# Dealing the bias generator's relu planes anew between two engines, and loading and casting the second unit's q, k and v later

## The chip, the cores and the metric

The kernel runs on one core of a Trainium2 chip. The metric is the device time of one execution in microseconds, given as the median of three runs. Five engines work side by side, each through its own instructions in order: PE (matrix multiply and transpose), DVE (vector), ACT (activation functions and copies), POOL (general) and SP (which here issues every DMA). Two engines meet only at semaphores: an instruction that waits holds up all that stands behind it on its engine.

## What is computed

For 4 batches and 8 heads, with 576 positions and 64 features a head, the reference computes attention with a learned relative bias, and then a two-layer network on the result:

```python
scores = scale * np.matmul(q, k.transpose(0, 1, 3, 2))
x = (np.log1p(np.abs(rel)) / psi_i)[..., None]
h = np.maximum(x @ w1 + b1, 0.0)
bias = h @ w2
scores = scores + bias.transpose(2, 0, 1)[None, :, :, :]
attn = softmax(scores)
y = attn @ v
g = leaky_relu(y @ w_in)
out = g @ w_out
```

The bias depends on positions and heads alone: it is made once, at the start, and serves all four batches.

## The kernel before

The work has three stages. The **generator** makes the bias rows in 36 tiles of 16 rows of positions (the list `GEN` is their order). A tile needs four *relu planes* of 304 to 576 columns. `gen_r` makes each plane on ACT or on DVE (L113, L115), as the string `plan[g]` says; `plan` is worked out ahead by a loop that gives each plane to the engine with the smaller running load (L93 to L103). The planes live in a ring of nine buffers (tag `r`), so a plane can be begun only once the plane nine places before it has gone through PE. `gen_mm` multiplies the four planes with the second layer's weights on PE (L126), `gen_ev` scales the product into an SBUF row tile with two ACT instructions (L133, L134) and has SP write it to one of five DRAM tensors (L145). `gen_tick` runs the three in a staggered way. After certain tiles it calls `load_bias`, which reads a finished group of rows back as the bias of 128 query positions (L164 to L170); the last group, "3", is read when all rows are written.

The **attention** stage goes over 16 units (a pair of heads and a batch), with nine tiles each, in the order `KINDS` = A0 B0 A1 B1 M A2 B2 A3 B3. `step(n)` issues tile n: the scores on PE (`qk_mm`), the sum with the bias and the row's extreme on DVE (L265, `softmax_a`), exp on ACT (L273), and, three tiles later, transposes of the probabilities (L307), copies of them (L323, L316) and the product with v (L342, `pv`). After tiles M and B3 `recip` takes the reciprocal of the sums on DVE (L279, L280) and spreads it on POOL (L283 to L286). Unit 0 multiplies q and k as they are loaded (L236). Every later unit multiplies split values (L242): `split_hi` casts q and k on DVE (L195, L200), `split_lo` takes the rest on POOL (L207, L210), q in two halves and k in two halves; the first two matmuls of a tile use q and the cast k, the last two the rest of k. The table `SPL` says behind which tile of unit u the pieces for unit u + 1 are issued. `load_unit(u)` has SP load q and k (two halves each, L180), `load_v(u)` v (L186, L188); units 0 and 1 are loaded at the start of the program (L501 to L503), unit u + 2 from within unit u.

The third stage is the network (L461 to L497). No scheduler moves anything: each engine gets its instructions in the order in which the program issues them. SP's are in one queue, with the waits on semaphores in place.

Of the kernel before, what the change touches and what calls it, by code (L numbers as in the profile page):

```python
# [25 lines left out]
KINDS = ["A0", "B0", "A1", "B1", "M", "A2", "B2", "A3", "B3"]  # L26
GEN = [16, 17] + list(range(16)) + [34, 35] + list(range(18, 26)) + list(range(33, 25, -1))
SPL = {1: [(0, "q")], 2: [(1, "q", 0)], 3: [(1, "q", 1)], 4: [(0, "k")], 5: [(1, "k", 0)], 7: [(1, "k", 1)]}
GEN_AT = [39] * 9
LAG = 3  # L30
BLK = 512
# [5 lines left out]
def attention_ffn(ctx: ExitStack, tc: tile.TileContext, qt, kt, vm, vt, wi, wo, cst, out):  # L37
# [39 lines left out]
    def gen_setup():  # L77
        cut = 214 + S - 16 * GEN[0]
        for c in (slice(0, cut), slice(cut, 214 + S)):
            nc.sync.dma_start(out=cs[:, c], in_=cst[:, c])  # L80
        nc.vector.memset(warm[:], 0.0)
        nc.scalar.activation(out=warm[:], in_=warm[:], func=AF.Exp)
        nc.vector.tensor_scalar(out=bps[:], in0=psib, scalar1=b1c, scalar2=None, op0=ALU.mult)
        for c in (slice(0, cut - 214), slice(cut - 214, S)):
            nc.vector.tensor_scalar(out=ltw[:, c], in0=ltw[:, c], scalar1=w1c, scalar2=None, op0=ALU.mult)
        nc.gpsimd.tensor_scalar(out=w2d, in0=w2d, scalar1=8.0, scalar2=None, op0=ALU.mult)
# [3 lines left out]
    def gen_w(T):  # L90
        return max(S - 16 * T, 16 * T + 16)

    plan, load = [], {"a": 0.0, "v": 5.0}  # L93
    for T in GEN:
        w = gen_w(T)
        load["a"] += 0.84
        cost = {"a": 0.24 + 0.00072 * w, "v": 0.11 + 0.00056 * w}
        eng = ""
        for _ in range(4):
            e = min(cost, key=lambda c: load[c] + cost[c])  # L100
            load[e] += cost[e]
            eng += e
        plan.append("".join(sorted(eng)))  # L103

    def gen_r(g):
        T = GEN[g]
        w = gen_w(T)
        r = gr[T] = [None] * 4
        for q, c in enumerate(plan[g]):
            k = 4 * T + q  # L110
            t = gp.tile([128, S], F32, tag="r", name="r", bufs=9)
            if c == "a":
                nc.scalar.activation(out=t[:, :w], in_=ltw[:, :w], func=AF.Relu, bias=bps[:, k:k + 1])  # L113
            else:
                nc.vector.tensor_scalar(out=t[:, :w], in0=ltw[:, :w], scalar1=bps[:, k:k + 1], scalar2=0.0, op0=ALU.add, op1=ALU.max)  # L115
            r[q] = t

    def gen_mm(T):
        r = gr.pop(T)
        w = gen_w(T)  # L120
        pt = pstile("s" if w > 512 else "to"[T % 2])
        cuts = [(0, w)] if w <= 512 else [(0, w // 2), (w // 2, w)]
        o0 = 512 - w // 2 if w > 512 else 0
        for a, b in cuts:
            for q in range(4):
                nc.tensor.matmul(pt[32 * q:32 * q + 32, o0 + a:o0 + b], w2d, r[q][:, a:b], start=True, stop=True)  # L126
        gps[T] = pt, o0

    def gen_ev(T):
        pt, o0 = gps.pop(T)  # L130
        R, F = 16 * T + 15, S - 16 * T
        e = e_b[GEN.index(T) % len(e_b)]
        nc.scalar.activation(out=e[:, R:W], in_=pt[:, o0:o0 + F], func=AF.Copy, scale=ips[:, T:T + 1])  # L133
        nc.scalar.activation(out=e[:, 0:R], in_=pt[:, o0 + R:o0:-1], func=AF.Copy, scale=ips[:, T:T + 1])  # L134
        if T < 16:
            c, r0 = str(T // 8), 16 * (T % 8)
        elif T < 18:
            c, r0 = "M", 16 * (T - 16)
        elif T < 34:
            c, r0 = str(2 + (T - 18) // 8), 16 * ((T - 18) % 8)  # L140
        else:
            c, r0 = "M", 32 + 16 * (T - 34)
        a = r0 * H * PIT + 1
        dst = scr[c][a:a + 16 * (H * PIT + 1)].rearrange("(i x) -> i x", i=16)[:, 0:H * PIT].rearrange("i (h p) -> i h p", h=H)[:, :, 0:W]
        nc.sync.dma_start(out=dst, in_=e)  # L145

    def gen_tick(g):
        if g + 1 < 36:
            gen_r(g + 1)
        if 0 <= g < 36:  # L150
            gen_mm(GEN[g])
        if 0 <= g - 1 < 36:
            gen_ev(GEN[g - 1])
        for c in {16: "0", 24: "1", 27: "M", 34: "2", 37: "3"}.get(g, ()):
            load_bias(0, c)

    bias = {}

    def load_bias(hp, c):
        n = 64 if c == "M" else 128  # L160
        rows = scr[c][0:n * H * PIT].rearrange("(i h p) -> i h p", h=H, p=PIT)[:, :, 16:16 + S]
        if c == "M":
            t = ap.tile([128, S], F32, tag="biasM", name="biasM", bufs=2)
            nc.sync.dma_start(out=t[0:64, :], in_=rows[:, 2 * hp, :])  # L164
            nc.sync.dma_start(out=t[64:128, :], in_=rows[:, 2 * hp + 1, :])
        else:
            t = ap.tile([128, 2, S], F32, tag="bias", name="bias", bufs=5)
            nc.sync.dma_start(out=t[:, 0, :], in_=rows[:, 2 * hp, :])
            nc.sync.dma_start(out=t[:, 1, 64:S], in_=rows[:, 2 * hp + 1, 0:512])
            nc.sync.dma_start(out=t[:, 1, 0:64], in_=rows[:, 2 * hp + 1, 512:S])  # L170
        bias[hp, c] = t
# [3 lines left out]
    def load_unit(u):  # L175
        hp, b = divmod(u, B)
        q_, k_ = raw_b[u % 2] if u else raw_0
        for t, src in ((q_, qt), (k_, kt)):
            for p in (0, 64):
                nc.sync.dma_start(out=t[p:p + 64], in_=src[hp, b])  # L180
        raw[u] = (q_, k_)

    def load_v(u):
        hp, b = divmod(u, B)
        v_ = ap.tile([128, 4, 128], F32, tag="v", name="v", bufs=3)
        nc.sync.dma_start(out=v_[:], in_=vm[hp, b])  # L186
        for h in range(2):
            nc.sync.dma_start(out=vt_b[u % 3][64 * h:64 * h + 64, h, :], in_=vt[hp, b, h])  # L188
        vv[u] = v_
# [200 lines left out]
    def w_alloc(pool, m):  # L390
        wt[m] = [pool.tile([128, DM], F32R, name=f"w{c}{m}") for c in ("ih", "il", "oh", "ol")]

    def x_alloc(pool, i):
        for k in range(KC):
            xs[i, k] = [pool.tile([128, BLK], F32R, name=f"x{c}{i}{k}") for c in "hl"]
# [102 lines left out]

    with tc.manual_schedule():
        gen_setup()  # L500
        for u in range(2):  # L501
            load_unit(u)
            load_v(u)  # L503
        done = -1
        early_ops = []
        for n in range(NTILE + LAG + 6):
            u, i = divmod(n, 9)
            if u == 0:
                while done < GEN_AT[i]:
                    gen_tick(done)  # L510
                    done += 1
            if n == 9:
                gen.close()
                early = ctx.enter_context(tc.tile_pool(name="early", bufs=1, side="right"))
                x_alloc(early, 0)
                w_alloc(early, 0)
                early.tile([128, 24], F32, name="gap")
                stage, stage_y = ExitStack(), ExitStack()
                pools["s"] = stage.enter_context(tc.tile_pool(name="stage", bufs=1, side="right"))
                pools["y"] = stage_y.enter_context(tc.tile_pool(name="stage_y", bufs=1, side="right"))  # L520
            step(n)
            if n == 13:
                w_fill()
                for m in range(EARLY):
                    early_ops += [(w_abs, m, h) for h in range(2)]
                    early_ops += [(w_bits, m, h, k) for k in range(4) for h in range(2)]
                    if m == 0:
                        early_ops += [(w_hi, 0, h) for h in range(2)] + [(w_lo, 0, h, nc.vector) for h in range(2)]
            for _ in range({0: 3, 4: 3}.get(i, 0) if n >= 18 else 0):
                if early_ops:  # L530
                    f, *args = early_ops.pop(0)
                    f(*args)
            if n == NTILE + 2:
                ffn1(0, 0)
            if u < HP * B:
                if u % B == B - 1 and u // B + 1 < HP:
                    c = {1: "0", 2: "1", 3: "M", 4: "2", 6: "3"}.get(i)
                    if c:
                        load_bias(u // B + 1, c)
                if u + 1 < HP * B:  # L540
                    for f, *args in SPL.get(i, ()):
                        (split_hi, split_lo)[f](u + 1, *args)
                if i == 8 and u + 2 < HP * B:
                    load_v(u + 2)
# [97 lines left out]
```

## Time and profile before

| | |
|---|---|
| median of 3 runs | 703.01 us (702.84 to 703.58) |
| the profiled execution | 702.97 us |
| its span, first to last instruction | 701.2 us |
| PE busy, share of the span | 691.4 us, 99% |
| weight loads of PE busy | 542.1 us, 77% |
| DVE busy | 368.2 us, 53% |
| ACT busy | 362.9 us, 52% |
| POOL busy | 109.9 us, 16% |

Between the span and the time lie 1.8 us that belong to no instruction. The shares are means over three stages with different limits, so each stage has to be read by itself: the generator fills about the first 50 us, the attention ends near 305 us, and the rest is the network. A busy PE is one whose matmuls overlap in the records, not one that runs at its peak. What counts for an engine in order is what its waiting instruction waits for, and what stands behind it.

### The profile page before, as it was taken

To read this page: it belongs to the slowest core of one execution; us is meant where nothing else is said; L and a number is where in the kernel's file an instruction comes from. 1 tells how busy PE (TensorE), PEld (TensorE's weight loads), DVE (VectorE), ACT (ScalarE), POOL (GpSimd) and SP (SyncE) were. 2 spreads that over 40 slices of the span, in tenths; PEclk is the share of its full clock that TensorE was granted. 3 is DMA by queue.
4 is the path that set the end of the run, shared out by engine and by line. 5 is a ranking of instruction groups with operands and counts; after the bars stand their busy time and mean duration, and the time that the engine had idled before them with its cause. 6 is when DMAs were issued, how large, how long until landed. Compare 5 with 4: busy or idle time off the path is not lost.

```text
span 701.2 us, 11179 instructions
## 1 busy us (share of the span) xinstructions
PE 691.4 (99%) x4192; PEld 542.1 (77%) x4192; DVE 368.2 (53%) x872; ACT 362.9 (52%) x792; POOL 109.9 (16%) x139
## 2 busy tenths in 40 slices
PE   7999999999999999999999999999999999999997
PEld 3446788777877778768888888888888888888896
DVE  6997788988898898569993111121111211111211
ACT  8998878787788777765653212222122222222221
POOL 0005434543454345100000000000000000000000
PEclk9999999999999999999999999999999999999999
DMA  9996779548738752005540100001000010000100
GB/s 230 338 303 191 206 185 241 141 109 231 205 98 246 217 145 73 1 1 156 175 121 1 60 1 0 1 1 60 1 0 1 1 60 1 0 1 1 60 1 31
DMA packets 30262, 68.26 MB, mean 97 GB/s; under 512 B 8192, under 2 KB 8320, under 8 KB 30208
## 3 DMA queue, kind: packets, MB, share of 16 engines
q1 hardware_dynamic: 30208, 67.54, 33.5%
q8 instruction: 33, 0.54, 0.3%
q14 instruction: 21, 0.17, 0.1%
HBM read 51.92 MB, written 15.61 MB: 96 GB/s over the span
## 4 chain that ended last, share of the span: by engine, by line
PE 95%; DMA 1%; ACT 1%; DVE 1%; issue 0%; SPq 0%; DVEq 0%
PE ps_o L461 14%; PE ps_t L461 13%; PE ps_o L342 12%; PE ps_s L242 10%; PE ps_s L489 9%; PE ps_s L488 9%; PE ps_s L487 9%; PE ps_t L307 9%; PE ps_o L126 2%; PE ps_t L126 2%; PE ps_s L227 1%; PE ps_s L126 1%; PE ps_o L296 1%; PE ps_o L325 1%; ACT r L113 1%; DMA scr<-x 1%
## 5 line engine op out<-in xcount | busy, mean ns | idle before, releaser
L476 DVE TENSOR_TENSOR gl<-g,gh 128x512 fp32r<-128x512 f32 (+1 forms) x80 | 51.0, 638 | 266.2 <-ACT g L470 266.2
L489 PE MATMUL ps_s<-woh,gl 128*128 128x512 f32 x288 | 112.2, 389 | 0.3 <-DVE gl L476 0.3
L487 PE MATMUL ps_s<-woh,gh 128*128 128x512 f32 x288 | 112.3, 390 | 0.0
L488 PE MATMUL ps_s<-wol,gh 128*128 128x512 f32 x288 | 112.2, 390 | 0.0
L265 DVE CUSTOM_DVE_ANT_0 p<-ps_s,bias 128x576 f32<-128x576 f32 x128 | 94.4, 753 | 30.4 <-PE ps_s L242 26.7
L273 ACT ACTIVATE p<-p,mx 128x576 f32<-128x576 f32 x128 | 99.8, 779 | 5.5 <-DVE mx L265 4.8
L323 ACT COPY PT<-ps_t 128x512 f32<-128x512 f32 x128 | 73.8, 577 | 47.5 <-PE ps_t L307 47.5
L242 PE MATMUL ps_s<-ks,qs 128*128 128x288 f32 x480 | 93.7, 317 | 0.2 <-DVE mx L265 0.2
L469 ACT ACTIVATE gh<-ps_o 128x512 fp32r<-128x512 f32 (+1 forms) x39 | 21.5, 552 | 126.5 <-PE ps_o L461 126.5
L469 ACT ACTIVATE gh<-ps_t 128x512 fp32r<-128x512 f32 (+1 forms) x39 | 21.5, 551 | 112.0 <-PE ps_t L461 111.9
L242 PEld LDWEIGHTS ps_s<-ks,qs 128*128 128x128 f32 x480 | 67.6, 189 | 13.6 <-issue 6.1
L307 PE MATMUL ps_t<-ident,p 128*128 128x128 f32 x512 | 77.5, 274 | 0.0
L342 PE MATMUL ps_o<-PT,v 128*64 128x288 f32 x512 | 69.2, 412 | 0.0
L307 PEld LDWEIGHTS ps_t<-ident,p 128*128 128x128 f32 x512 | 61.0, 140 | 9.1 <-issue 8.2
L489 PEld LDWEIGHTS ps_s<-woh,gl 128*128 128x128 f32 x288 | 54.1, 188 | 11.9 <-DVE gl L476 0.7
L488 PEld LDWEIGHTS ps_s<-wol,gh 128*128 128x128 f32 x288 | 54.1, 188 | 10.8
L487 PEld LDWEIGHTS ps_s<-woh,gh 128*128 128x128 f32 x288 | 54.1, 188 | 10.7
L461 PE MATMUL ps_t<-xh,wil 128*128 128x512 f32 (+1 forms) x156 | 57.3, 367 | 0.0
L461 PE MATMUL ps_o<-xh,wil 128*128 128x512 f32 (+1 forms) x156 | 57.3, 367 | 0.0
L461 PE MATMUL ps_o<-xl,wih 128*128 128x512 f32 (+1 forms) x156 | 57.3, 367 | 0.0
L461 PE MATMUL ps_t<-xl,wih 128*128 128x512 f32 (+1 forms) x156 | 57.3, 367 | 0.0
L461 PE MATMUL ps_o<-xh,wih 128*128 128x512 f32 (+1 forms) x156 | 57.3, 367 | 0.0
(111 smaller groups left out, 1081.4 us busy)
## 6 DMA issues: line engine op xcount, KB each, us to landing
raw<-kt SPq DMA_DIRECT2D x32, 304.0 KB, 5.9
raw<-qt SPq DMA_DIRECT2D x32, 288.0 KB, 4.4
raw<-wi SPq DMA_DIRECT2D x16, 512.0 KB, 4.9
raw<-wo SPq DMA_DIRECT2D x16, 512.0 KB, 3.6
scr<-x SPq DMA_DIRECT2D x21, 295.5 KB, 4.6
bias<-scr SPq DMA_DIRECT2D x16, 288.0 KB, 4.6
out<-x SPq DMA_DIRECT2D x18, 256.0 KB, 2.1
v<-vm SPq DMA_DIRECT2D x16, 256.0 KB, 5.7
```

The lines of the kernel that those rows point to most:

```text
L242: nc.tensor.matmul(s_[:, S0 + HS * hh:S0 + HS * hh + HS], qs[:, c0:c0 + 128], ks[:, k0 + HS * hh:k0 + HS * hh + HS], start=(j == 0), stop= ...
L265: nc.vector.tensor_tensor_reduce(out=p, in0=s_[:, S0:S0 + S], in1=bt, scale=-0.125, scalar=3.4e38, op0=ALU.add, op1=ALU.min, accum_out=i)
L273: nc.scalar.activation(out=p, in_=p, func=AF.Exp, bias=i, scale=-1.0, accum_out=sm)
L307: nc.tensor.transpose(t0[:, 128 * jb:128 * jb + 128], p[:, p0 + 128 * jb:p0 + 128 * jb + 128], ident[:])
L323: nc.scalar.copy(out=PT[:, g, 0:8, c].rearrange("p (j h) c -> p j h c", h=2)[:, :, h, :], in_=t0[:].rearrange("p (j c) -> p j c", j=4))
L342: nc.tensor.matmul(o[64 * h:64 * h + 64, 0:HS], l, r, start=(jb == 0), stop=(jb == 4))
L461: nc.tensor.matmul(h_[:, :N], w, x[:, :N], start=(j == 0), stop=(j == len(mms) - 1))
L469: nc.scalar.activation(out=gh[:, :N], in_=h_[:, :N], func=AF.Prelu, alpha=0.01)
L476: nc.vector.tensor_sub(gl[:, :N], g[:, :N], gh[:, :N].bitcast(F32))
L487: nc.tensor.matmul(o, gh[:, c], wt[m][2][:], start=(m == 0), stop=False)
L488: nc.tensor.matmul(o, gh[:, c], wt[m][3][:], start=False, stop=False)
L489: nc.tensor.matmul(o, gl[:, c], wt[m][2][:], start=False, stop=(m == MF - 1))
```

## The change

It makes three edits. The planner's start loads and costs are given other numbers, and so other planes go to ACT and to DVE. Unit 1 is no longer loaded at the start: its `load_unit` and `load_v` are called in the generator's tick 37, behind the reading of bias group "3". And while unit 0 runs, a table `SPL1` takes the place of `SPL`: q's cast is issued behind tile M (index 4), the first half of q's rest and k's cast behind A2 (5), the second half of q's rest behind B2 (6), both halves of k's rest behind A3 (7).

```diff
 SPL = {1: [(0, "q")], 2: [(1, "q", 0)], 3: [(1, "q", 1)], 4: [(0, "k")], 5: [(1, "k", 0)], 7: [(1, "k", 1)]}
+SPL1 = {4: [(0, "q")], 5: [(1, "q", 0), (0, "k")], 6: [(1, "q", 1)], 7: [(1, "k", 0), (1, "k", 1)]}
...
-    plan, load = [], {"a": 0.0, "v": 5.0}
+    plan, load = [], {"a": -1.6, "v": 0.0}
     for T in GEN:
         w = gen_w(T)
-        load["a"] += 0.84
-        cost = {"a": 0.24 + 0.00072 * w, "v": 0.11 + 0.00056 * w}
+        load["a"] += 0.80
+        cost = {"a": 0.187 + 0.00083 * w, "v": 0.11 + 0.00057 * w}
...
         for c in {16: "0", 24: "1", 27: "M", 34: "2", 37: "3"}.get(g, ()):
             load_bias(0, c)
+        if g == 37:
+            load_unit(1)
+            load_v(1)
...
-        for u in range(2):
-            load_unit(u)
-            load_v(u)
+        load_unit(0)
+        load_v(0)
...
-                    for f, *args in SPL.get(i, ()):
+                    for f, *args in (SPL if u else SPL1).get(i, ()):
                         (split_hi, split_lo)[f](u + 1, *args)
```

The diff shows the numbers of the planner and not the deal that comes of them. DVE now makes 117 of the 144 planes (115 before), ACT 27 (29 before). The first planes on DVE, at the start of the program, where `r` is a plane and the last number its columns. Before:

```order
L85 TENSOR_SCALAR cs<-cs 128x256
L115 TENSOR_SCALAR r<-cs,bps 128x304
L115 TENSOR_SCALAR r<-cs,bps 128x576 x3
L115 TENSOR_SCALAR r<-cs,bps 128x560 x3
L115 TENSOR_SCALAR r<-cs,bps 128x544 x3
```

Now:

```order
L86 TENSOR_SCALAR cs<-cs 128x256
L116 TENSOR_SCALAR r<-cs,bps 128x320
L116 TENSOR_SCALAR r<-cs,bps 128x304 x4
L116 TENSOR_SCALAR r<-cs,bps 128x576 x3
L116 TENSOR_SCALAR r<-cs,bps 128x560 x3
L116 TENSOR_SCALAR r<-cs,bps 128x544 x4
```

Four of the small planes of the first two tiles, and one of 544 columns, have gone from ACT to DVE; later tiles give planes back.

SP's queue around the end of the generator. `scr_76` holds the rows of group "3", `raw_84` and `raw_85` are the buffers of unit 1's q and k, `raw_82` and `raw_83` those of unit 2. Before:

```order
L145 DMA scr_76<-x_2_71 16x8x591 [waits DMAHW5_49,Activation_49]
L145 DMA scr_76<-x_3_72 16x8x591 [waits DMAHW6_49,Activation_49]
L168 DMA bias<-scr_76 128x576 [waits DMAHW6_49,DMAHW5_49,DMAHW7_49,DMAHW1_49,DMAHW0_49]
L169 DMA bias<-scr_76 128x512
L170 DMA bias<-scr_76 128x64
L180 DMA raw_82<-qt 64x1152 [waits DMAHW2_49]
L180 DMA raw_82<-qt 64x1152 [waits DMAHW3_49]
L180 DMA raw_83<-kt 64x1216 [waits DMAHW4_49]
```

Now:

```order
L146 DMA scr_76<-x_2_71 16x8x591 [waits DMAHW6_49,Activation_49]
L146 DMA scr_76<-x_3_72 16x8x591 [waits DMAHW7_49,Activation_49]
L172 DMA bias<-scr_76 128x576 [waits DMAHW6_49,DMAHW2_49,DMAHW7_49,DMAHW1_49,DMAHW0_49]
L173 DMA bias<-scr_76 128x512
L174 DMA bias<-scr_76 128x64
L184 DMA raw_84<-qt 64x1152 [waits DMAHW3_49]
L184 DMA raw_84<-qt 64x1152 [waits DMAHW4_49]
L184 DMA raw_85<-kt 64x1216 [waits DMAHW5_49]
L184 DMA raw_85<-kt 64x1216
L190 DMA v<-vm 128x512
```

Unit 1's loads stand directly behind the reading of group "3", whose first instruction waits for the landing of the group's writes; that is the place that unit 2's loads had. Unit 2's follow behind unit 1's.

DVE from tile M of unit 0 on. The ISA rows are the sum with the bias and its extreme, `qs` and `ks` the cast q and k. Before:

```order
L265 ISA pM,mx<-ps_s,biasM 128x576 [waits DMAHW2_49,DMAHW1_49,PE_49]
L265 ISA mx 128x1
L200 CAST ks_782<-raw_85 128x1216
L265 ISA p,mx<-ps_s,bias 128x576 [waits DMAHW2_49,PE_49]
L265 ISA mx 128x1
L279 TENSOR_SCALAR sm<-sm 128x5 [waits Activation_49]
L280 RECIPROCAL sm<-sm 128x5 [waits DVE_49]
```

Now:

```order
L269 ISA pM,mx<-ps_s,biasM 128x576 [waits DMAHW3_49,DMAHW2_49,PE_49]
L269 ISA mx 128x1
L199 CAST qs_101<-raw_84 128x1024 [waits DMAHW4_49,DMAHW3_49]
L269 ISA p,mx<-ps_s,bias 128x576 [waits PE_49]
L269 ISA mx 128x1
L283 TENSOR_SCALAR sm<-sm 128x5 [waits Activation_49]
L284 RECIPROCAL sm<-sm 128x5 [waits DVE_49]
L204 CAST ks_821<-raw_85 128x1216 [waits DMAHW6_49,DMAHW5_49]
```

q's cast stood between tiles B0 and A1 and now stands between M and A2. It has got a wait for the landing of two DMAs, which are q's two halves. k's cast has got such a wait too. On POOL the spreading of M's reciprocal now comes ahead of q's rest, where it came behind it.

## Rows read from the trace of the kernel before

**Rows 1.** Busy time by stretch: us, then PE, PEld, DVE, ACT, POOL, clock, DMA share, GB/s.

```profile
61.00:76.60 15.60, 15.60 (x128) 12.21 (x128) 12.36 (x33) 12.04 (x30) 6.48 (x10) 1.00 0.77 182
76.60:92.20 15.60, 15.60 (x129) 12.20 (x128) 12.22 (x35) 12.90 (x30) 7.25 (x10) 1.00 0.67 194
```

**Rows 2.** The chain of waits behind the generator: start, length, what.

```profile
52.76 4.00 DMA scr<-x
...
56.91 2.86 DMA bias<-scr
...
59.91 0.76 DVE p L265
...
60.73 0.79 PE ps_s L242 x4
```

**Rows 3.** DVE's relu planes as one group: busy, mean ns, idle time before them.

```profile
L115 DVE TENSOR_SCALAR r<-cs,bps 128x560 f32<-128x560 f32 (+17 forms) x115 | 42.0, 450 | 2.9 <-PE ps_t L126 1.4 <-PE ps_s L126 1.1 <-PE ps_o L126 0.3
```

**Rows 4.** DVE's timeline in the generator: start, length, idle time before in brackets.

```profile
5.97 1.41 DVE L115 TENSOR_SCALAR r<-cs,bps 128x576 f32<-128x576 f32 x3 [1.43 <-PE ps_t L126]
...
10.22 38.79 DVE L115 TENSOR_SCALAR r<-cs,bps 128x544 f32<-128x544 f32 x108 [1.13 <-PE ps_s L126]
```

**Rows 5.** ACT's timeline: the generator's last eviction.

```profile
50.31 0.61 ACT L134 ACTIVATE x<-ps_t,cs 128x431 f32<-128x431 f32 x1
```

**Rows 6.** SP's timeline of issues, from the last two writes on.

```profile
52.13 1.17 SPq L145 DMA_DIRECT2D scr<-x  x2
...
58.24 1.15 SPq L180 DMA_DIRECT2D raw<-qt  x2
59.43 1.24 SPq L180 DMA_DIRECT2D raw<-kt  x2
```

**Rows 7.** DMA issues, each second half: KB, us from the issue's start to landing.

```profile
raw<-qt SPq DMA_DIRECT2D x1, 288.0 KB, 5.1
...
raw<-kt SPq DMA_DIRECT2D x1, 304.0 KB, 6.5
```

**Rows 8.** DVE's timeline in unit 0.

```profile
52.10 0.69 DVE L195 CAST qs<-raw 128x1024 fp32r<-128x1024 f32 x1
52.70 0.75 DVE L265 CUSTOM_DVE_ANT_0 p<-ps_s,bias 128x576 f32<-128x576 f32 x1
...
54.30 0.76 DVE L265 CUSTOM_DVE_ANT_0 pM<-ps_s,biasM 128x576 f32<-128x576 f32 x1 [0.16 <-PE ps_s L227]
...
56.88 0.17 DVE L279 TENSOR_SCALAR sm<-sm 128x5 f32<-128x5 f32 x1
```

**Rows 9.** POOL's timeline: the rest of q, the spreading, the rest of k.

```profile
52.93 2.51 POOL L207 TENSOR_TENSOR qs<-raw,qs 64x512 fp32r<-64x512 f32 x2 [48.88 <-DVE qs L195]
57.41 0.40 POOL L283 COPY rb<-sm 128x256 f32<-128x256 f32 x1 [1.98 <-DVE sm L280]
...
58.18 2.92 POOL L210 TENSOR_TENSOR ks<-raw,ks 128x576 fp32r<-128x576 f32 x2
...
74.74 1.43 POOL L210 TENSOR_TENSOR ks<-raw,ks 128x576 fp32r<-128x576 f32 x1
```

**Rows 10.** PE's timeline: first matmuls; scores of A3 of unit 0, of B0 of unit 1.

```profile
4.68 2.13 PE L126 MATMUL ps_t<-r,cs 128*32 128x320 f32 x7 [4.68 <-ACT r L113]
...
57.51 0.76 PE L236 MATMUL ps_s<-raw,raw 64*128 64x288 f32 x4
...
64.58 0.79 PE L242 MATMUL ps_s<-ks,qs 128*128 128x288 f32 x4
```

**Rows 11.** One matmul form from 7.9 to 9.9 us and from 28.5 to 30 us.

```profile
L126 PE MATMUL ps_s<-r,cs 128*32 128x288 f32 x16 | 2.5, 687 | 0.0
...
L126 PE MATMUL ps_s<-r,cs 128*32 128x288 f32 x5 | 1.2, 416 | 0.0
```

**Rows 12.** Busy time by stretch behind the last matmul; the clock follows POOL.

```profile
697.60:699.00 1.40, 0.00 (x0) 0.00 (x0) 0.03 (x1) 0.59 (x1) 0.00 (x0) 1.00 0.36 133
699.00:701.00 2.00, 0.00 (x0) 0.00 (x0) 0.00 (x0) 0.00 (x0) 0.00 (x0) 0.75 0.45 169
```

## The prediction

> **What bounds the kernel now.** I read the busy times by stretch first, to find where PE sets the pace, then the chain of waits for what holds it up before that, and then the timeline of each engine on that chain.
>
> From 61 us on PE leaves no gap: two units in a row take 15.6 us each and PE is busy for all of both, while DVE and ACT have some 3 us of slack in each [rows 1]. What PE has to do from there to the end is the same in both kernels, so the end moves by as much as PE's place at the start of unit 1 moves, unless a new wait appears later. That place is the scores of unit 1's first tile, at 60.73 [rows 2]. Ahead of it the chain runs through the generator's last write (52.76, 4.00 long), the reading of bias group "3" behind its landing (56.91), and tile A3 on DVE at 59.91 [rows 2]. So what matters is what the change does to two things: the generator's end, and everything that DVE, POOL and PE need before unit 1.
>
> **The generator (the new deal).** DVE makes 115 planes in 42.0 us and is idle for 2.9 us between them [rows 3], all of it before 10.22; from there 108 planes follow each other without a gap for 38.79 us, 0.36 us a plane [rows 4]. ACT's last eviction ends at 50.92 [rows 5], behind DVE's last plane at 49.0. With the new deal DVE has four planes more at once and works where it stood idle. Of the 2.9 us I leave some 0.8: the ring of nine still holds its first 576-column plane until the first plane has gone through PE, at 5.97 [rows 4], and four small planes more bring DVE only to about 5.6; and about 0.4 us more where PE, slow at that time (below), is late again. The two planes that DVE makes more in all cost 0.7 us. The gain is 2.9 - 0.8 - 0.7 = 1.4 us at DVE's end, and I carry it to ACT's last eviction, the last write and the reading of group "3". Bounds: 0.5 us, if PE and ACT hold the ring up more often, and 2.2 us, if no idle time is left.
>
> Taking unit 1's seven transfers out of SP's queue at the start saves nothing that I can see: there are 19 row tiles, so no eviction waits for a write before the 20th. Were a late write what holds that one up, the transfers' 1.5 MB would be worth some tenths.
>
> **The loads.** This is the costly edit. SP issues in order, and group "3" waits for the landing of the last write: the last two writes are issued at 52.13, the next issue is at 56.91 [rows 2, 6]. Whatever stands behind it cannot leave earlier. In the kernel before that place belongs to unit 2's q and k, so their rows tell when unit 1's will land. q's second half is issued at 58.24 + 1.15 / 2 = 58.8 and lands 5.1 us later, at 63.9; k's second half is issued at 60.05 and lands 6.5 us later, at 66.55 [rows 6, 7]. With the gain of 1.4 us that is 62.5 and 65.15. Before, the same data had been there since the start and its cast ran at 52.10 without a wait [rows 8].
>
> **The casts.** DVE now meets q's cast directly behind tile M. M is done at 55.0 [rows 8]; without q's cast ahead of it (0.6 us) and with the gain it is done near 53.0. There DVE stands for 62.5 - 53.0 = 9.5 us, and behind it tiles A2, B2, A3 and B3, on which ACT and PE wait. PE has the scores of two tiles ahead, no more, since it has two score buffers.
>
> From q's landing on, in the times of the kernel before (the gain comes off at the end):
>
> - q lands at 63.9; cast 0.6 (52.10 to 52.70, rows 8): 64.5.
> - A2's sum and extreme, 0.7 (a reduction is 0.75 with some overlap, rows 8): 65.2.
> - M's reciprocal, from 56.88 on DVE to 57.41 on POOL, 0.5 [rows 8, 9]: 65.7.
> - The spreading on POOL, 57.41 to 58.18, 0.8 [rows 9]: 66.5. It now stands ahead of q's rest in POOL's queue.
> - q's rest, both halves, 2.5 [rows 9]: 69.0.
> - The first half of k's rest, 1.4 [rows 9]: 70.4. k's cast fits beside: k lands at 66.55 and a cast of some 1.1 us ends before 69.0.
>
> Then PE can begin the second pair of matmuls of unit 1's first tile. Before, it did so in the middle of the 0.79 us that begin at 60.73, at 61.1. So PE's place moves by 70.4 - 61.1 = 9.3 us, less 1.4: **7.9 us later**. PE's other work up to there, tiles A3 and B3 and their transposes, fits into the time in which POOL works, if the clock is full. The products with v and the next tiles then run at the old pace; unit 2's loads, now behind unit 1's, land some 6 us later than before and are needed 8 us later, so they bring no second stall.
>
> **PE's clock.** PE will do nothing for about 9 us. That is far longer than anything inside the old kernel. The old trace shows both ends of the matter: the same 288-column matmul takes 687 ns at 8 us, 3 us behind the first matmul at 4.68, and 416 ns at 29 us [rows 10, 11], and behind the last matmul (ended 697.6) the granted clock is still 1.00 until 699 and 0.75 on average over the next two microseconds, that is 1.2 GHz for half of them [rows 12]. So I take it that PE comes back at 1.2 GHz when A2 frees its buffer, near 63.8, and is at 2.4 GHz again about as late behind that as at the start: slow ones reach to 9.9 there [rows 11], 5.2 us behind the first, and I take a little more, 5.6. Its work from A3's scores to the second pair is 61.1 - 57.5 = 3.6 us at full clock with 0.2 of waits [rows 2, 10], 3.4 net, so 6.8 us at half. From 63.8 to 69.4 it does 5.6 of these, and the rest takes 0.6: the second pair begins at 70.0 and not at 70.4 - 1.4 = 69.0. I add **1.0 us**. Bounds: 0, if the clock stays up; and 5.1, if it stays down to the end of the first product with v, that is 1.6 us by the second pair (63.8 + 6.8 = 70.6) and 3.5 us more for the work between 61.1 and 64.58 [rows 10].
>
> The Trainium skill's page "TensorE: Matmul & The Clock Gate", in the section "What's actually happening", says that the throttled clock is the default and that activity releases it. By it the 1.0 us stands; a sum without it would give 710.9. The end of the trace agrees (0.75 once PE stands); that a stall inside the kernel does the same, no row here shows.
>
> **Sum.** 9.3 - 1.4 + 1.0 = 8.9 us on the profiled execution's 702.97, which is at the median of the runs (703.01): **711.9 us**. A measurement of this kernel can tell about 0.2%, 1.4 us, from no change.
>
> **The rivals.**
>
> 1. *The clock stays at 1.2 GHz through the first product with v* (chance 0.13). Same stall, with 1.6 to 5.1 us in place of 1.0: 712.5 to 716, taken at 714.5. For it: PE's work behind the stall is broken up by waits for DVE and POOL, where at the start PE had one matmul behind the other. Against it: at half clock these waits fill with work.
> 2. *The new deal brings next to nothing* (0.10): the planner's loads balance on paper, but the ring and PE set the pace, or the run of writes on SP and the DMA engines cannot go faster. With a gain of 0 to 0.5 us the time is 712.8 to 713.3. Against it: DVE's idle time lies early and is plain.
> 3. *Faster: q and k are there when DVE comes to them* (0.03). Then only the gain is left, at best 703.0 - 1.4 = 701.6. It decides at one point: q's second half must have landed when M is done, near 53.0, and so be issued by 47.9. The order of SP puts it behind group "3", whose wait ended at 56.9; the generator would have to end some 9 us earlier, and DVE alone has 42.0 us of planes.
> 4. *No change to be seen* (0.02): stall and gain cancel. It would take a q that lands about 8 us earlier than by the rows, and nothing in them points there.
>
> My forecast, the stall with a clock that falls or not and comes back by unit 1's first tiles, has 0.72.
>
> **How the numbers follow.** The low end takes the gain at 2.2 and no loss by the clock: 702.97 + 9.3 - 2.2 = 710.1, and 0.1 off for rounding, 710.0. The high end takes a gain of 0.5 with 2.7 us by the clock, about the middle of its bounds: 702.97 + 9.3 - 0.5 + 2.7 = 714.5. That holds my forecast, rival 2 and half of rival 1. Slower by over 0.2%: 0.72 + 0.13 + 0.10 = 0.95; within 0.2%: 0.02; faster: 0.03.
>
> **What would show it.** Right, step by step: the writes' last landing near 55.4 instead of 56.76; on DVE a wait of 9 to 10 us before q's cast, released by the DMA of q; on PE one idle stretch of about that length between 54 and 64; a granted clock under 1.00 there; POOL's spreading ahead of q's rest, and k's rest as what PE waits for at unit 1's first tile; and from there 15.6 us a unit as before. Wrong: q's cast with a wait under 3 us; unit 1 beginning before 66; or a second stall in unit 1 or 2, for loads that come late one after the other, which would put the time over 714.

## The result and the profile after

The changed kernel takes **712.9 us** (median of four executions, 711.87 to 713.62) against 703.13 for the kernel before: a ratio of 1.0133, 95% interval 1.0121 to 1.0145 (the ratios on record are not the quotients of the medians). That is slower by 9.8 us. The forecast was 711.9, in a range of 710.0 to 714.5. The execution that was profiled is the shortest of the four: 711.87 us, span 710.1, that is 8.90 us over the profiled execution before.

From PE's side the change is one idle stretch and what follows it. PE's timeline of the changed kernel (start, length, line, in brackets the idle time before and what ended it):

```profile
55.49 0.27 PE L329 MATMUL ps_o<-ident,p 128*128 128x128 f32 x1
64.11 1.33 PE L240 MATMUL ps_s<-raw,raw 64*128 64x288 f32 x4 [8.34 <-DVE mx L269]
...
67.96 0.76 PE L240 MATMUL ps_s<-raw,raw 64*128 64x288 f32 x4 [0.62 <-DVE mx L269]
...
69.06 0.51 PE L246 MATMUL ps_s<-ks,qs 128*128 128x288 f32 x2
69.91 0.53 PE L246 MATMUL ps_s<-ks,qs 128*128 128x288 f32 x2 [0.35 <-POOL ks L214]
...
70.92 2.16 PE L346 MATMUL ps_o<-PT,v 128*64 128x288 f32 x16
...
73.50 0.80 PE L246 MATMUL ps_s<-ks,qs 128*128 128x288 f32 x4
```

The last line is unit 1's tile B0. It began at 64.58 [rows 10] and begins at 73.50, 8.92 us later: the whole difference of the two profiled executions (8.90) is in front of it. Behind it nothing is lost. Busy time by stretch (us, then PE, PEld, DVE, ACT, POOL, clock, DMA share, GB/s):

```profile
56.00:64.00 8.00, 0.00 (x0) 0.00 (x0) 1.31 (x4) 0.00 (x0) 0.00 (x0) 0.77 0.87 228
64.00:67.20 3.20, 3.09 (x12) 2.07 (x12) 2.17 (x6) 1.34 (x3) 2.69 (x5) 0.50 1.05 259
67.20:73.50 6.30, 5.33 (x38) 3.18 (x38) 4.35 (x14) 4.69 (x11) 4.50 (x4) 1.00 0.66 155
73.50:89.10 15.60, 15.60 (x128) 12.20 (x126) 11.69 (x31) 12.40 (x30) 8.08 (x10) 1.00 0.66 194
89.10:104.70 15.60, 15.60 (x128) 12.21 (x126) 13.61 (x37) 12.33 (x29) 6.94 (x8) 1.00 0.44 103
```

The first stretch has no PE, ACT or POOL at all while the DMA engines are busy for 0.87 of it. The last two are units of 15.6 us without a gap, as before [rows 1].

What PE waits for is DVE, and DVE waits for q. DVE's timeline, from the generator's last planes to k's cast:

```profile
13.26 33.94 DVE L116 TENSOR_SCALAR r<-cs,bps 128x496 f32<-128x496 f32 x96 [0.18 <-PE ps_s L127]
...
62.69 0.69 DVE L199 CAST qs<-raw 128x1024 fp32r<-128x1024 f32 x1 [9.44 <-DMA raw<-qt]
...
65.36 1.88 DVE L204 CAST ks<-raw 128x1216 fp32r<-128x1216 f32 x1 [1.00 <-DMA raw<-kt]
```

The deal itself works: the planes end at 47.20 and not at 49.0 [rows 4], and DVE's idle time between them is 0.6 us where 2.9 stood [rows 3]:

```profile
L116 DVE TENSOR_SCALAR r<-cs,bps 128x304 f32<-128x304 f32 (+17 forms) x117 | 42.3, 442 | 0.6 <-PE ps_t L127 0.3 <-PE ps_s L127 0.2
```

ACT's last eviction, too, comes 1.8 us earlier (48.49 + 0.61 = 49.10 against 50.92, rows 5):

```profile
48.49 0.61 ACT L135 ACTIVATE x<-ps_t,cs 128x431 f32<-128x431 f32 x1
```

SP hands on less than half of that:

```profile
48.58 0.80 SPq L172 DMA_DIRECT2D bias<-scr  x1
49.43 1.03 SPq L173 DMA_DIRECT2D bias<-scr  x1
50.52 1.12 SPq L174 DMA_DIRECT2D bias<-scr  x1
51.74 1.17 SPq L146 DMA_DIRECT2D scr<-x  x2
56.06 0.33 SPq L172 DMA_DIRECT2D bias<-scr  x1
...
57.38 1.15 SPq L184 DMA_DIRECT2D raw<-qt  x2
```

The first three lines read bias group "2"; the last two writes stand behind them in SP's queue and leave at 51.74, only 0.4 us earlier than before [rows 6]. Group "3" follows at 56.06 (56.91 before, rows 2), and q and k behind it. In the kernel before, the reading of group "2" stood at the same place in SP's queue; there it began later and ended at 52.04:

```profile
49.92 1.00 SPq L168 DMA_DIRECT2D bias<-scr  x1
...
51.59 0.45 SPq L170 DMA_DIRECT2D bias<-scr  x1
```

POOL's work, with the spreading (L287) now ahead of q's rest (L211) and k's rest (L214):

```profile
64.42 0.40 POOL L287 COPY rb<-sm 128x256 f32<-128x256 f32 x1 [60.22 <-DVE sm L284]
...
65.32 3.04 POOL L211 TENSOR_TENSOR qs<-raw,qs 64x512 fp32r<-64x512 f32 x2
68.44 2.94 POOL L214 TENSOR_TENSOR ks<-raw,ks 128x576 fp32r<-128x576 f32 x2
```

q's rest takes 3.04 us where it took 2.51 [rows 9], and DVE's cast of k 1.88 where it took 1.11. The two overlap in both kernels, at different points. Before, k's cast (54.98 to 56.09) met the second half of q's rest, which ended at 55.44; now it meets the first half, which takes 1.27 us and ends at 66.59, and the cast ends at 67.24. Both times it ends 0.65 us behind the end of a POOL instruction. It does so in the profiles of experiments 1, 2 and 4 to 10 as well, wherever it began; in experiment 3, where it meets no part of q's rest, it takes 0.75. Where it meets the first half, the second half takes 1.82 us and not 1.27; where it meets the second, POOL loses nothing. So they look as if they took turns; no run was made to test that.

### The profile page after: what moved, and what is told of

Read it like the earlier page. It is cut to its first block, busy times and chain, and to the rows that moved or that the text cites. A ratio compares the mean times of both kernels' runs of the same rounds, so it can differ in the third digit from the quotient of the medians.

```text
span 710.1 us, 11176 instructions
## 1 busy us (share of the span) xinstructions
PE 690.6 (97%) x4192; PEld 541.2 (76%) x4192; DVE 369.4 (52%) x874; ACT 361.5 (51%) x790; POOL 110.4 (16%) x139
## 4 chain that ended last, share of the span: by engine, by line
PE 91%; DMA 3%; ACT 3%; DVE 2%; issue 1%; SPq 0%; POOL 0%; DVEq 0%; POOLq 0%; ACTq 0%
PE ps_o L465 13%; PE ps_t L465 13%; PE ps_o L346 12%; PE ps_s L246 10%; PE ps_s L493 9%; PE ps_s L491 9%; PE ps_s L492 9%; PE ps_t L311 9%; PE ps_s L231 1%; PE ps_o L329 1%; PE ps_o L300 1%; DMA scr<-x 1%; DMA raw<-kt 1%; ACT r L114 1%; PE ps_s L127 1%; ACT x L134 1%
## 5 line engine op out<-in xcount | busy, mean ns | idle before, releaser
L311 PEld LDWEIGHTS ps_t<-ident,p 128*128 128x128 f32 x512 | 61.1, 140 | 9.0 <-issue 7.3
L465 PE MATMUL ps_t<-xh,wih 128*128 128x512 f32 (+1 forms) x156 | 57.3, 367 | 0.0
```

Source lines behind the costliest of these rows:

```text
L311: nc.tensor.transpose(t0[:, 128 * jb:128 * jb + 128], p[:, p0 + 128 * jb:p0 + 128 * jb + 128], ident[:])
L465: nc.tensor.matmul(h_[:, :N], w, x[:, :N], start=(j == 0), stop=(j == len(mms) - 1))
```

## The experiments

The theory: the loss comes from the landing of q and k behind group "3", hardly from the place of the casts; the deal is a small gain; the clock adds something of its own. The rivals: the loss is due to DVE's order (casts ahead of A2); the deal brings nothing; the clock decides most. Medians below are over all executions of a run, ratios are to the kernel before on the same chip. Where two runs were made on different chips, only their distances from the kernel before can be compared.

**1. The deal alone.** The planner's new numbers in the kernel before; loads and casts as they were.

```diff
-    plan, load = [], {"a": 0.0, "v": 5.0}
+    plan, load = [], {"a": -1.6, "v": 0.0}
-        load["a"] += 0.84
-        cost = {"a": 0.24 + 0.00072 * w, "v": 0.11 + 0.00056 * w}
+        load["a"] += 0.80
+        cost = {"a": 0.187 + 0.00083 * w, "v": 0.11 + 0.00057 * w}
```

> The changed kernel with unit 1's loads put back to the start and its casts to their old tiles: only the new deal of relu planes is left. Theory: the deal ends DVE's planes 1.8 us earlier, but SP's run of issues passes on only some 0.8 us of it (last landing near 56.0 instead of 56.76), so the time is 0.8 us under before, 702.3. Forecast as it was on record: 1.4 us under, 701.6. Rival, the deal is worth nothing or costs: 703.0 or more.

Measured: 702.58 us, ratio 0.999 (0.9981 to 0.9998), 0.8 us less than before. DVE and ACT win far more than that: the last eviction ends at 49.35, 1.6 us earlier. The chain of waits shows where it stays:

```profile
52.33 4.17 DMA scr<-x
...
56.66 2.83 DMA bias<-scr
```

The last write still leaves at 52.33 (52.76 before) and group "3" is read at 56.66 (56.91 before): the end of the generator is set by SP and the DMA engines as well. In this profile unit 1 begins only 0.29 us earlier (60.44 against 60.73); the 0.8 is a difference of medians, and the interval goes from 0.1 to 1.3 us.

**2. The old deal with the late loads and casts**, that is the changed kernel without its first edit.

> The changed kernel with the old planner numbers: the late loads and late casts alone. Theory: everything from the last write's landing on is 0.8 us later than in the changed kernel, 712.7 to 714.4, by the clock. Rival, the early transfers that were taken out of the queue helped the generator: under 712.

Measured: 713.67 us, ratio 1.0156 (1.0141 to 1.0171). The other two edits cost 10.3 us (713.67 less 703.38, the median of the kernel before on this chip). The changed kernel lies 9.8 and 9.5 us (experiment 6) over the kernel before in its two runs, so by the medians the deal is worth 0.5 to 0.8 us with the loads late; by the ratios it is some 1.5, and the intervals overlap. The generator's last eviction ends at 50.78 here, 0.14 us before its time in the kernel before: in this profile, taking seven transfers out of the start is worth no more.

**3. The casts late, the loads early:** experiment 1 with `SPL1` for unit 0.

```diff
-                    for f, *args in SPL.get(i, ()):
+                    for f, *args in (SPL if u else SPL1).get(i, ()):
```

> The changed kernel with unit 1's loads put back to the start; the casts stay behind tiles M, A2, B2 and A3 of unit 0. Theory: late data alone makes the stall, so with q and k there the late casts cost nothing: the same time as the deal alone, 702.3, no wait before q's cast. Rival, the later place of the casts costs by itself because k's rest on POOL ends late: unit 1 begins 1 to 3 us later than with the deal alone, 703.3 to 705.

Measured: 702.67 us, ratio 0.9998 (0.9988 to 1.0008), 0.1 us over experiment 1 by the medians and 0.5 by the means. What the changed kernel loses is the late data, not the place of the casts. But the place may have a risk: eight of its twelve executions took 702.1 to 702.9 us and four 704.4 to 704.9 (one of eleven is above 704 in experiment 1, and two of 29 of the kernel before). The profiled one, 704.45, is of the four; whether the short ones lack what it shows is not known. In it PE waits 2.08 us for k's rest on POOL, and the first product with v then takes 3.85 us, with a granted clock of 0.50 from 62 to 65 us, where it takes 2.16 at the full clock:

```profile
60.56 0.77 PE L243 MATMUL ps_s<-ks,qs 128*128 128x288 f32 x4 [2.08 <-POOL ks L211]
...
61.81 3.85 PE L343 MATMUL ps_o<-PT,v 128*64 128x288 f32 x16
```

**4. The changed kernel, all casts behind tile B3.** DVE is then free for A2, B2, A3 and B3 while q is on its way.

```diff
-SPL1 = {4: [(0, "q")], 5: [(1, "q", 0), (0, "k")], 6: [(1, "q", 1)], 7: [(1, "k", 0), (1, "k", 1)]}
+SPL1 = {8: [(0, "q"), (1, "q", 0), (1, "q", 1), (0, "k"), (1, "k", 0), (1, "k", 1)]}
```

> The changed kernel with all of unit 1's casts and rests behind tile B3 of unit 0: the data come as late as there, but DVE goes on with A2, B2, A3 and B3 meanwhile. Theory: unit 1 still waits for q and k, but q's rest no longer stands behind M's spreading, and k's cast and rest follow their data: the second pair of unit 1's first tile begins near 67.9 instead of 69.9, 2 us under the changed kernel. The late data then account for all that is left, some 7 us over before. Rival, DVE's place in the queue is what costs: 6 us or more are won back.

Measured: 712.3 us, ratio 1.0138 (1.0122 to 1.0153), 0.6 us under the changed kernel by the medians and, by the ratios (1.0135 there, experiment 6), not under it at all: less than expected. PE's timeline tells why:

```profile
66.69 0.82 PE L246 MATMUL ps_s<-ks,qs 128*128 128x288 f32 x2 [7.77 <-DVE ks L204]
68.13 0.85 PE L246 MATMUL ps_s<-ks,qs 128*128 128x288 f32 x2 [0.63 <-POOL ks L214]
...
69.98 2.82 PE L346 MATMUL ps_o<-PT,v 128*64 128x288 f32 x16
...
73.21 0.80 PE L246 MATMUL ps_s<-ks,qs 128*128 128x288 f32 x4
```

The second pair of unit 1's first tile begins at 68.13, 1.8 us earlier than in the changed kernel. But PE has only just come back: each pair takes 0.8 us and not 0.5, the product 2.82 and not 2.16, and of the 1.8 us 0.3 are left at tile B0.

**5. Unit 1's loads ahead of group "3"**, still behind the last writes.

```diff
+        if g == 37:
+            load_unit(1)
+            load_v(1)
         for c in {16: "0", 24: "1", 27: "M", 34: "2", 37: "3"}.get(g, ()):
             load_bias(0, c)
-        if g == 37:
-            load_unit(1)
-            load_v(1)
```

> The changed kernel with unit 1's loads ahead of the reading of bias group 3 instead of behind it, still behind all writes: they no longer stand behind a wait for a landing. Theory: q's second half leaves SP 4.4 us earlier and lands near 58.1, k near 60.9; 4 to 4.5 us under the changed kernel, 708.0 to 708.8. Rival, the DMA engines are full with writes until 56 anyway, so the loads land hardly earlier, and group 3 comes 5 us later: within 1 us of the changed kernel.

Measured: 707.44 us, ratio 1.0064 (1.0051 to 1.0077): 5.5 us of the 9.5 by which the changed kernel is slower on this chip (712.91 less 703.38, experiment 6) come back by an exchange of two calls. q's cast has half of its wait left:

```profile
58.04 0.69 DVE L199 CAST qs<-raw 128x1024 fp32r<-128x1024 f32 x1 [5.30 <-DMA raw<-qt]
```

This settles the main cause: a wait at the head of SP's queue holds back transfers that have nothing to do with it. The other 4 us stay: the loads still leave behind the last writes, q from 51.57 on.

**6. The changed kernel once more**, for its spread and a second profile.

> The changed kernel once more, beside the next three on one chip: 711.9 to 713.6. Theory of the spread: the stretch at 1.2 GHz differs between executions, so a longer time goes with a lower mean granted clock. Rival: the times differ at one clock.

Measured: 712.91 us (711.6 to 713.65), ratio 1.0135 (1.0121 to 1.0149). The execution profiled here took 713.15, 1.3 us more than the one shown above, though q's cast begins at the same time (62.61 against 62.69) and k's too (65.39 against 65.36). What differs is the clock. Busy time by stretch, first in the execution above, then in this one:

```profile
64.00:67.00 3.00, 2.89 (x12) 2.07 (x12) 1.97 (x5) 1.34 (x3) 2.49 (x5) 0.50 1.08 267
67.00:70.00 3.00, 2.03 (x13) 1.08 (x11) 2.96 (x9) 2.06 (x6) 2.92 (x3) 0.96 0.99 229
70.00:73.50 3.50, 3.50 (x27) 2.10 (x28) 1.60 (x6) 2.63 (x7) 1.77 (x2) 1.00 0.37 90
```

```profile
64.00:67.00 3.00, 2.97 (x12) 2.07 (x12) 1.86 (x3) 1.34 (x3) 2.57 (x5) 0.50 1.06 246
67.00:70.00 3.00, 2.37 (x11) 1.36 (x9) 2.96 (x9) 2.11 (x5) 2.92 (x3) 0.50 1.01 230
70.00:73.50 3.50, 3.50 (x21) 2.68 (x21) 1.44 (x6) 2.70 (x6) 1.68 (x2) 0.66 0.36 81
```

The clock column reads 0.50, 0.96, 1.00 in the one and 0.50, 0.50, 0.66 in the other. So the scores of unit 1's first tile, the transposes and the start of the product run at 1.2 GHz, and tile B0 begins at 74.84:

```profile
69.92 1.31 PE L246 MATMUL ps_s<-ks,qs 128*128 128x288 f32 x4
...
72.22 2.20 PE L346 MATMUL ps_o<-PT,v 128*64 128x288 f32 x16
...
74.84 0.80 PE L246 MATMUL ps_s<-ks,qs 128*128 128x288 f32 x4
```

**7. PE kept busy in the stall.** 72 transposes of the identity, which nobody reads, ahead of A3's scores.

```diff
+            if n == 7:
+                idle_t = pstile("t")
+                for _ in range(72):
+                    nc.tensor.transpose(idle_t[:, 0:128], ident[:], ident[:])
             step(n)
```

> The changed kernel with 72 transposes of the identity ahead of tile A3's scores on PE, into a buffer that nothing reads, 7.8 us of work in the 8.3 us in which PE stood idle. Theory: the granted clock stays at 1.00, unit 1 waits for POOL alone, and the time is 711.5 in every run, with a spread under 0.5 us. Rival, the clock has no part in it: median and spread as in the changed kernel, 712.9 and 1.7 us.

Measured: 712.76 us (712.63 to 713.2), ratio 1.0136 (1.0122 to 1.015). The spread is smaller, the median is not lower: a miss. The clock stays at 1.00 through the stall, and falls behind it:

```profile
67.35 0.76 PE L240 MATMUL ps_s<-raw,raw 64*128 64x288 f32 x4 [2.02 <-DVE mx L269]
...
69.29 0.85 PE L246 MATMUL ps_s<-ks,qs 128*128 128x288 f32 x2 [0.34 <-POOL ks L214]
...
71.14 2.93 PE L346 MATMUL ps_o<-PT,v 128*64 128x288 f32 x16
...
74.48 0.80 PE L246 MATMUL ps_s<-ks,qs 128*128 128x288 f32 x4
```

PE is busy for 0.65 us of the 2 us from 66 on, and the granted clock is 0.83 in 68 to 70 and 0.50 in 70 to 72: now it is the first product with v that runs slowly. The fall was moved, not removed.

**8. PE kept busy in all three gaps.**

```diff
-            if n == 7:
+            if n in (7, 8, 9):
                 idle_t = pstile("t")
-                for _ in range(72):
+                for _ in range({7: 72, 8: 18, 9: 4}[n]):
```

> The changed kernel, with PE given identity transposes (nobody reads them) in all three of its gaps: 72 ahead of A3's scores, 18 ahead of B3's, 4 between the two halves of unit 1's first tile. With 72 alone PE then stood for 2.0 us ahead of B3's scores, and the granted clock was 0.50 in 70 to 72 us. Theory (the two executions of the changed kernel that were profiled differ by the clock alone: 0.50 until 67.2 us in one and until about 72 in the other, 1.3 us apart): with the clock at 1.00 all the way unit 1's first tile waits only for POOL, its second product tile begins near 73.5 us, and every execution comes out near the shorter of the two, 711.6 to 712.2, with a spread under 1 us. Rival (the clock falls whatever PE did, or the later executions are longer for another reason): 712.6 to 713.2 as before, second product tile at 74.3 or later.

Measured: 712.81 us (711.96 to 713.98), ratio 1.0132 (1.0116 to 1.0147). As a forecast of the time this is a miss, median and spread alike. The clock is 1.00 in all stretches from 52 to 74 us, as the theory said, and the profiled execution is the longest of its four all the same, 713.98:

```profile
64.35 0.69 DVE L199 CAST qs<-raw 128x1024 fp32r<-128x1024 f32 x1 [10.96 <-DMA raw<-qt]
```

q's cast begins 1.66 us later than in the changed kernel's profile. SP read group "2" from 49.37 to 52.36 here: no longer than there (2.99 us against 3.06), but from 0.8 us later on. The last writes left at 52.46, 0.7 later, and group "3" at 57.05, 1.0 later; q took the other 0.67 us on its way from there. So there is a second cause of the spread, on the way of the data: SP's issues, the writes' landing and the loads themselves take differently long from one execution to another. The four executions differ by 2.0 us, all with a mean granted clock of 1.0, so the clock explains only a part. Over all profiles with late loads and the casts in this order, the time from the start of q's cast to the start of tile B0 sorts the two:

| kernel | q's cast | tile B0 | between | clock |
|---|---|---|---|---|
| changed | 62.69 | 73.50 | 10.81 | back ahead of the product with v |
| old deal (2) | 64.47 | 75.29 | 10.82 | back ahead of it |
| loads ahead of "3" (5) | 58.04 | 68.85 | 10.81 | back ahead of it |
| changed, again (6) | 62.61 | 74.84 | 12.23 | low up to the product |
| one gap filled (7) | 62.08 | 74.48 | 12.40 | low in the product |
| three gaps filled (8) | 64.35 | 75.68 | 11.33 | 1.00 throughout |

With the clock back in time the distance is the same to 0.01 us; where it is not, 1.4 to 1.6 us come on top. In (8) the extra transposes themselves stand in the way. The 18 are done before B3's scores can start (5.28 us behind q's cast, 5.27 in the changed kernel), but they take one of the two buffers of the transposes, and so PE waits for ACT's copy:

```profile
71.00 0.66 PE L311 MATMUL ps_t<-ident,p 128*128 128x128 f32 x4 [0.62 <-ACT PT L317]
```

The four ahead of unit 1's first tile (not between its halves, as I had put it) take 0.36 us more. That 1.00 throughout gives 10.81 without such filling wasn't seen.

The profile's chain of waits in the changed kernel goes by k's landing (65.27) and not by q's. The table speaks for q: in the first three rows k's cast begins 2.67, 3.10 and 3.18 us behind q's, and the distance stays the same.

**9. A better order of reading.** Experiment 1 with group "2" read behind the last writes.

```diff
-        for c in {16: "0", 24: "1", 27: "M", 34: "2", 37: "3"}.get(g, ()):
+        for c in {16: "0", 24: "1", 27: "M", 37: "23"}.get(g, ()):
```

> The new deal, loads and casts as before, and the reading of bias group 2 moved behind the last two writes. Theory: the last two writes, which stood 3.3 us behind their evictions on SP, now leave at once and land near 53; group 3 lands before tile A3 wants it, DVE runs through unit 0 without the wait there, and unit 1 begins 3 to 3.5 us earlier than in the kernel before: 699.5 to 700.2. Rival, group 2 comes late for tile A2 and takes the place of group 3 as the wait: 701.5 or more.

Measured: **701.68 us**, ratio 0.998 (0.9971 to 0.9989): faster than both kernels by a little, 1.7 us under the one before and less than I expected. SP's timeline:

```profile
45.47 5.12 SPq L146 DMA_DIRECT2D scr<-x  x5
50.64 0.60 SPq L169 DMA_DIRECT2D bias<-scr  x1
...
54.28 0.32 SPq L169 DMA_DIRECT2D bias<-scr  x1
```

All writes have left by 50.6 and group "3" is read at 54.28, 2.6 us earlier than before. Tile B0 of unit 1 begins at 62.59 (64.58 before), 2.0 us earlier. The rest goes to tile A2, which waits 1.17 us on DVE for group "2".

**10. That order in the kernel before**, with the old deal.

> The kernel before with one edit: the bias rows of group 2 are read behind the last writes, together with group 3, instead of ahead of them. It separates the two parts of the version that came out at 701.68 (new deal and this order). Theory (in the old deal SP is held up little by group 2, its last two writes leave 2.6 and 1.8 us behind their evictions, against 3.4 and 3.3 in the new deal): the order is worth 0.3 to 1.0 us alone, 702.3 to 703.0 us, and the new deal gives the rest. Rival (the order gives it all, the deal nothing): 701.7 us as with both.

Measured: 702.7 us, ratio 0.9992 (0.9984 to 1.0001), 0.5 us less than before. So by the medians the deal alone gives 0.8, the order alone 0.5, both 1.7; the intervals are some 0.6 us wide to either side, and that of the order alone holds no change. The profiles say more. Unit 1's first scores on PE in the kernel before, with the deal alone, with the order alone and with both:

```profile
60.73 0.79 PE L242 MATMUL ps_s<-ks,qs 128*128 128x288 f32 x4 [0.17 <-DVE mx L265]
60.44 0.80 PE L243 MATMUL ps_s<-ks,qs 128*128 128x288 f32 x4 [1.45 <-DVE mx L266]
60.71 0.78 PE L242 MATMUL ps_s<-ks,qs 128*128 128x288 f32 x4
58.76 0.78 PE L243 MATMUL ps_s<-ks,qs 128*128 128x288 f32 x4
```

Before, two limits lay 0.17 us apart: PE's own work, which begins when the generator ends, and the reading of group "3", for which DVE and then PE wait. The deal alone moves the first (PE then waits 1.45 us), the order alone the second (PE waits no more, and next to nothing is gained: tile B0 begins at 64.54 against 64.58), and only both together move the start of the unit. Group "3" is read at 55.93 with the order alone and at 54.28 with both: with group "2" out of the way, 1.65 of the deal's 1.8 us come through SP.

## Why the prediction was right, and which terms were not

**The stall** came as forecast: a wait of 9.44 us before q's cast (9.5 forecast), released by q's DMA; PE idle from 55.8 to 64.1; the spreading ahead of q's rest; k's rest as what PE waits for at unit 1's first tile, at 69.91 (70.0 forecast, but with 1.0 us for the clock that this execution did not need); no second stall and 15.6 us a unit behind it. Experiments 3 and 5 show that it is the landing behind group "3" that costs, not the place of the casts.

**The gain of the deal**, 1.4 us, failed at one step: "I carry it to ACT's last eviction, the last write and the reading of group "3"". At DVE's end and at ACT's last eviction it was 1.8 us. At the reading of group "3" it was 0.85, since SP was still reading group "2"; by the medians it is 0.8 in experiment 1 and 0.5 to 0.8 in experiment 2. The bounds (0.5 to 2.2) held it. SP's timeline of the kernel before has that reading directly ahead of the two writes (rows 6 begin behind it); I followed the engines and not the queue. Experiments 9 and 10 show the step: with the reading out of the way, 1.65 us come through. The writes' last landing came at 55.98 and not near 55.4.

**The landing of q.** Its second half left at 57.95 and landed at 62.6, 4.6 us later and not 5.1: this gave 0.5 back.

**POOL's and DVE's shares.** From q's landing to the second pair I summed 6.5 us. It was 7.3: q's rest took 3.04 and not 2.5, because DVE's cast of k fell between its halves; I had counted it as free ("k's cast fits beside"). The other 0.3 lies in handovers between engines.

**The clock**, 1.0 us, cost nothing in the first profile, where it was back at 67.2 and PE then waited for POOL anyway, and some 1.3 us in the second. With nothing for the clock, the terms as measured give 9.3 - 0.85 - 0.5 + 0.8 = 8.75, the 8.8 by which the second pair moved (61.1 to 69.91). The median lies 1.0 us over this execution and over the forecast. The mean granted clock of the four executions was 0.994, 0.990, 0.992 and 0.990, the first being the profiled one: as far as a mean tells, most of them are like the second profile. It does not tell all: two executions of experiment 2 took 713.68 and 713.66 us at 0.995 and 0.992. I chose a clock that is back in time as the likeliest, with a price taken in full; what happens more often lies between that and rival 1, in which the clock is low through the whole product and which I priced at 714.5. The Trainium skill's page "TensorE: Matmul & The Clock Gate", section "What's actually happening", has the low clock as the default that activity lifts; the runs agree, inside a kernel as well: 0.50 behind a stall of 8.3 us, 1.00 in the stall that was filled.

**Luck.** That the sum (711.9) meets the profiled execution (711.87) is luck: the gain was 0.55 too large and POOL's share 0.8 too small, the way of q 0.5 and the clock 1.0 too dear, and these cancel to 0.15 us.

**Rival 2** (the deal brings next to nothing, 0 to 0.5 us) is not borne out by the medians (0.5 to 0.8), but the interval of experiment 1 reaches down to 0.1, so it is not excluded. One of its reasons, the run of writes on SP, is what halves the gain. **Rivals 3 and 4** needed q some 8 us earlier, and nothing brought it there.

## What to carry to other kernels

In this kernel a transfer's time of arrival was set above all by what stood ahead of it in its issuing queue: before a load is moved behind a write, look for the first issue there that waits for a landing, and take the rows of whatever stood behind it so far as the arrival. When a plan gives an engine less to do, follow the gain through the queues down to the consumer, since a second limit close behind the first takes the rest. Where PE stands for some microseconds, reckon its work behind the stall at both levels of the clock; in two executions of the changed kernel the lower one lasted some 3 and 8 us behind PE's return.

## What the runs showed of the hardware that was not expected

- Two executions of the same kernel, with q's and k's casts at the same times within 0.1 us, differed by 1.3 us through the stretch for which the granted clock stayed at 0.50.
- The clock also fell behind short waits, but not behind each: in experiment 7 behind a wait of 2.02 us (0.50 in 70 to 72 us), in experiment 3 behind one of 2.08 us, where the product with v took 3.85 us and not 2.16; in experiment 8, behind one of 2.00 us and with the gaps after it filled, it stayed at 1.00.
- Where POOL's subtraction and DVE's cast of k meet, the cast ends 0.65 us behind the end of a POOL instruction, wherever it began (eleven profiles): it took 1.88 us in the changed kernel, begun 0.04 us behind POOL's start, and 1.05 in experiment 8, begun 0.87 behind it. Where it falls between POOL's two halves, these take 3.04 us and not 2.51.
- The same three issues on SP, those that read group "2", took 3.06 us in the changed kernel's first profile (48.58 to 51.64), 2.99 in experiment 8, 2.12 before (49.92 to 52.04) and 1.56 in experiment 7 (47.70 to 49.26).
